# Three stages on one core: products in another order, two shared PSUM banks, other distances between the streams

## The chip, the core and the metric

The kernel runs on one core of a Trainium2 chip. The metric is the device time of one execution in microseconds (us), lower is better. A profile shows one further execution with every instruction's start and end. TensorE (PE) multiplies, and its weight loads (PEld) run beside it; VectorE (DVE), ScalarE (ACT) and GpSimd (POOL) do the elementwise work, the first two of them also out of PSUM, the matmuls' target of eight banks; SyncE (SP) issues all DMAs. Each engine takes its instructions in a fixed order, and semaphores make it wait for others.

## What is computed

Eight sequences of 576 tokens pass three stages. All tensors are float32.

```python
# 1: attention in chunks of 64 tokens, 8 heads of 64
scores = scale * np.matmul(q_c, k_c.transpose(0, 1, 2, 4, 3))
attn = softmax(scores); x = attn @ v_c            # -> x: (8, 576, 512)
# 2: gated block
h = np.maximum(x @ w_in, 0.0)
u, v = (h[..., :d_ff // 2], h[..., d_ff // 2:])
v_s = np.einsum('ts,bsd->btd', w_spatial, layernorm(v)) + b_spatial[None, :, None]
x = (u * v_s) @ w_out
# 3: a low-rank mix over the tokens, then two channel products
u = x + (x.transpose(0, 2, 1) @ U @ V).transpose(0, 2, 1)
out = u + np.maximum(u @ w_ch1, 0.0) @ w_ch2      # 512 -> 2048 -> 512
```

## The kernel before

Every float32 operand is split into a high and a low float16 part, and a product is three matmuls (`mm3`, lines 167 to 169): high by high, high by low, low by high. So TensorE's rows of almost every stage have these three lines, and the output tile tells them apart.

The work runs in four streams of Python generators. `gen_attn` takes 27 turns of attention (the first 9 run earlier by `gen_first`): scores into a tile `sp`, softmax, a transpose by DMA (`pt<-ph`), the second product into a tile `o`. `gen_moe(b)` does the gated block and the token mix of batch b. In PSUM tiles named `pb` it has, per batch, four or five v products of 512 columns (into `rz`), eight u products, eight spatial products and eight output products of 288 columns, four u stages of the low-rank mix (`tr`, into `ast`) and eight v stages (L762): four for the first part of the batch's tokens, which complete slice b of the channel stage, and four for the rest, which go to slice b + 1. After each, DVE adds (L763), ACT casts (L766) and POOL makes the low part (L767). `gen_sums(j)` forms, when slice j is complete, four sums of quarters of it (DVE L834 to L839, ACT L840, POOL L841), once for each half `kk` of its rows. `gen_quads` decodes packed weights for the channel stage, beside slice 0 only.

`gen_ch(j)` is the channel stage on slice j of 512 tokens, nine slices in all. Its first product is done as seven products of quarters (numbers 1 to 7, each six matmuls of 256 columns) instead of eight, with the sums as operands of 4 to 7. A slice has eight groups; in each, products 1, 6 and 2 go to the tile `pa` (one bank), and 5, 7, 3 and 4 to `pc` (one bank). ACT and DVE read them between the products (`q_e`, `q_v`, `q_z`) and make the hidden tile (L892, L893). Its second product, 24 matmuls of 512 columns into the four tiles `acc`, belongs to the group before and follows the seven. At a slice's end DVE reads `acc` into `ot` tiles (L942, L945; two buffers), ACT scales, and DMAs bring them out.

What sets the order is `Flow`: it runs the streams by an estimated clock. A stream that yields "pe" advances the clock and stays back by its pace times that cost; "wait" keeps it back for some ns, "need" until an event. The streams added first go first; the channel stage is last and fills what is left. A scheduler then places the instructions on each engine in the order that its own estimate gives, so the final order is not that of the code alone. A tile whose bank is in use by an earlier tile, or whose bank another engine still reads, waits.

PSUM before: four banks for `acc`, `pa` and `pc` one each (tags h0, h1), one for all `pb` tiles of the later batches (h2; `banks[0] = (2,)` before the streams start), and one for attention (pool `ps_a`).

Of the kernel before, what the change touches and what calls it, by code (L numbers as in the profile page):

```python
# [28 lines left out]

EARLY = (0, 0, 0, 0, 2, 1, 1)  # L30
FIRST_AT = 4
PACE_B = 0.8
PACES = (0.0, 0.0, 1.0, 1.0, 1.0, 1.0, 0.9, 0.9)
# [4 lines left out]
WA, WB, WC = 2500.0, 5500.0, 2500.0  # L38
# [54 lines left out]
def moe_kernel(  # L93
# [19 lines left out]
    ps_a = ctx.enter_context(tc.tile_pool(name="ps_a", bufs=1, space=PSUM))  # L113
# [4 lines left out]
    def b_psum(b):  # L118
        n = banks[0][banks[1] % len(banks[0])]
        banks[1] += 1  # L120
        return ps_h.tile([128, 512], F32, tag=f"h{n}", name="pb")
# [3 lines left out]
    NQ = NF // 2  # L125
# [404 lines left out]
    def gen_first(lo, hi):  # L530

        for i in range(lo, hi):
# [14 lines left out]
            tp = ps_a.tile([128, 4, 128], F32, tag="a", name="tp")  # L547
# [20 lines left out]
    def gen_attn(lo, hi):  # L568
# [5 lines left out]
        for i in range(lo, hi):  # L574
# [5 lines left out]
            sp = ps_a.tile([128, H, 64], F32, tag="a", name="sp")  # L580
# [20 lines left out]
            o = ps_a.tile([128, 4, 128], F32, tag="a", name="o")  # L601
# [21 lines left out]
    def gen_moe(b):  # L623
# [146 lines left out]
        for m in range(4):  # L770
# [17 lines left out]
            if m >= 1:  # L788
                if nxt == 2:
                    u_stage(m - 1)  # L790
                yield "pe", mmcost(128, 9)
            if m >= 2:
                v_stage(m - 2, 0, n1, b, 64 * b)
                yield "pe", mmcost(n1)
            yield "gap", 0
# [7 lines left out]
        for m in range(3, 4):  # L803
            v_stage(m, 0, n1, b, 64 * b)
            yield "pe", mmcost(n1)
        fl.done(("s", b, 0), 2500.0)
# [3 lines left out]
        for m in range(4):  # L810
            v_stage(m, n1, S - n1, b + 1, 0)
            yield "pe", mmcost(S - n1)
        fl.done(("s", b, 1), 2500.0)
# [10 lines left out]
    def gen_sums(j):  # L824
# [8 lines left out]
        for kk in range(2):  # L833
# [8 lines left out]
            yield "wait", 3000.0  # L842
        fl.done(("t", j), 3000.0)
# [7 lines left out]
    def gen_ch(j):  # L851
# [18 lines left out]

        for g in range(NQ + 1):
            n = j * NQ + g
            if g < NQ:
                if j == 0:
                    yield "need", ("wq", g)
                w = ws1_s[n % 3].rearrange("p a t (k m) -> p a t k m", k=2)
# [19 lines left out]

                product(1, pa[:, 0, :], True)
                nc.scalar.copy(out=q_e, in_=pa[:, 0, :])
                yield "pe", PQ
# [3 lines left out]
                product(5, pc[:, 0, :], True)  # L903
                add(q_v, pc[:, 0, :], q_e)
                yield "pe", PQ
                product(7, pc[:, 1, :], False)
                add(q_z[:, 2 * N2:3 * N2], pc[:, 1, :], q_v)
                yield "pe", PQ
                product(2, pa[:, 0, :], False)
# [3 lines left out]
                add(q_z[:, 0:N2], pc[:, 0, :], q_e)  # L913
                yield "pe", PQ
                product(4, pc[:, 1, :], False)
                w_load(0, n + 3)
                add(q_z[:, N2:2 * N2], pc[:, 1, :], q_e)
                parts(slice(N2, 4 * N2), q_z)
                yield "pe", PQ
            if g > 0:  # L920
                n -= 1
                w = ws2_s[n % 3]
                hd = hid_s[n % 2].rearrange("p a (f n) -> p a f n", f=2)
# [162 lines left out]
```

## Time and profile before

| | before |
|---|---|
| timed runs | 1480.81 and 1481.4 us, median 1481.11 |
| the profiled execution | 1483.17 us; span from first to last instruction 1481.4 us |
| mean granted TensorE clock | 0.933 of full |
| busy, share of the span | PE 1290.7 us (87%), DVE 770.9 (52%), POOL 593.1 (40%), ACT 561.7 (38%) |
| DMA | 185.47 MB, mean 125 GB/s |

PEclk is the granted clock of TensorE as a share of 2.4 GHz; it has two levels, 1.0 and 0.5, and a value between them is a mean over the stretch. Matmuls overlap in the profile: a row lasts longer than the distance to the next.

### The profile page before, as it was taken

The numbers are of one execution on the slowest core, as the hardware profiler recorded it, in microseconds if no ns is written. First come the engines' busy times: TensorE is split into PE (matmuls) and PEld (weight loads), VectorE is DVE, ScalarE is ACT, GpSimd is POOL, SyncE is SP. The second block draws the span as 40 slices with busy tenths as digits, with TensorE's granted clock in tenths as the row PEclk, the third lists the DMA queues.
The fourth block names the chain that finished last, engine by engine and source line by source line (L and its number), as shares of the span: only waits on it lengthen the run. The fifth ranks groups of instructions, "written<-read, shape, count | busy, mean of one in ns | idle before, by whom it ended". The sixth has DMA issues, their size and how long they took to land.

```text
span 1481.4 us, 24105 instructions
## 1 busy us (share of the span) xinstructions
PE 1290.7 (87%) x9604; PEld 869.6 (59%) x9604; DVE 770.9 (52%) x1427; ACT 561.7 (38%) x1127; POOL 593.1 (40%) x670
## 2 busy tenths in 40 slices
PE   8876688787899879997999699979996999589897
PEld 6564365554577637764776367746773676355554
DVE  6898877767634553446254635363325332733423
ACT  6665455444524532443245424333123212311111
POOL 3767686655615561545145525133113211500000
PEclk6897799888999979999999799989997999799999
DMA  8447443645434722562246313522333124234431
GB/s 263 132 141 232 135 130 123 198 127 182 137 115 143 177 73 86 148 151 105 83 128 163 109 65 100 146 94 82 104 102 91 65 93 127 90 118 139 149 118 43
DMA packets 119768, 185.47 MB, mean 125 GB/s; under 512 B 76132, under 2 KB 76772, under 8 KB 119656
## 3 DMA queue, kind: packets, MB, share of 16 engines
q1 hardware_dynamic: 119656, 183.93, 40.8%
q8 instruction: 75, 1.23, 0.3%
q14 instruction: 37, 0.30, 0.1%
HBM read 145.89 MB, written 20.97 MB: 113 GB/s over the span
## 4 chain that ended last, share of the span: by engine, by line
PE 53%; DVE 9%; POOL 5%; ACT 4%; DMA 3%; issue 2%; SPq 0%; ACTq 0%; POOLq 0%; DVEq 0%
PE acc L167 7%; PE acc L168 7%; PE acc L169 7%; PE pb L167 5%; PE pb L168 5%; PE pb L169 5%; PE pc L167 3%; PE pc L169 3%; PE pc L168 3%; PE pa L167 2%; PE pa L168 2%; PE pa L169 2%; POOL big L841 2%; DVE big L889 2%; DMA out_dram<-ot 2%
## 5 line engine op out<-in xcount | busy, mean ns | idle before, releaser
L889 DVE TENSOR_TENSOR big<-pc,big 128x256 f32<-128x256 f32 x288 | 121.5, 422 | 286.4 <-PE pc L169 282.0
L168 PEld LDWEIGHTS <-big 128*128 128x128 f16 x1584 | 156.3, 99 | 137.0 <-issue 51.9
L168 PE MATMUL acc<-big 128*128 128x512 f16 x576 | 219.1, 380 | 1.6 <-DVE big L893 1.5
L167 PEld LDWEIGHTS <-big 128*128 128x128 f16 x1584 | 156.2, 99 | 107.5 <-issue 29.9
L169 PE MATMUL acc<-big 128*128 128x512 f16 x576 | 218.6, 380 | 0.0
L169 PEld LDWEIGHTS <-big 128*128 128x128 f16 x1584 | 156.4, 99 | 86.3 <-issue 16.2
L167 PE MATMUL acc<-big 128*128 128x512 f16 x576 | 186.8, 383 | 4.7 <-ACT big L892 2.6
L167 PE MATMUL pc<-big 128*128 128x256 f16 x576 | 158.9, 276 | 26.3 <-DVE big L889 25.9
L169 PE MATMUL pc<-big 128*128 128x256 f16 x576 | 159.1, 276 | 0.0
L168 PE MATMUL pc<-big 128*128 128x256 f16 x576 | 158.9, 276 | 0.0
L719 POOL TENSOR_TENSOR gt<-g,gt 128x288 f16<-128x288 f32 x64 | 49.9, 781 | 240.7 <-ACT gt L718 240.3
L167 PE MATMUL pa<-big 128*128 128x256 f16 x432 | 120.5, 279 | 16.6 <-ACT big L840 7.5
L168 PE MATMUL pa<-big 128*128 128x256 f16 x432 | 120.2, 278 | 10.1 <-POOL big L841 9.0
L169 PE MATMUL pa<-big 128*128 128x256 f16 x432 | 120.4, 279 | 0.0
L893 DVE SCALAR_TENSOR_TENSOR big<-big 128x768 f16<-128x768 f32 x72 | 76.5, 1063 | 50.2 <-ACT big L892 50.0
L405 POOL TENSOR_TENSOR vbd<-vf,vbd 64x512 f16<-64x512 f32 x54 | 65.3, 1209 | 60.5 <-ACT vbd L404 52.9
L783 POOL TENSOR_TENSOR tr<-x,tr 128x64 f16<-128x64 f32 (+1 forms) x56 | 42.8, 785 | 114.7 <-ACT tr L780 66.2
L167 PE MATMUL pb<-gt,w 128*128 128x288 f16 x256 | 76.4, 298 | 14.1 <-DVE ast L751 5.1
L767 POOL TENSOR_TENSOR big<-x,big 128x512 f16<-128x512 f32 (+7 forms) x64 | 56.9, 896 | 77.5 <-ACT big L766 64.5
L892 ACT ACTIVATE big<-big 128x768 f16<-128x768 f32 x72 | 60.6, 842 | 68.2 <-DVE big L889 67.8
L167 PE MATMUL pb<-sp_m,vn 128*128 128x288 f16 x256 | 74.6, 291 | 13.4 <-DVE g L715 10.5
L892 ACT ACTIVATE big<-pa 128x256 f16<-128x256 f32 x72 | 27.5, 381 | 144.0 <-PE pa L169 135.1
(204 smaller groups left out, 3021.2 us busy)
## 6 DMA issues: line engine op xcount, KB each, us to landing
big<-wd SPq DMA_DIRECT2D x64, 896.0 KB, 4.7
big<-wd SPq DMA_DIRECT2D x64, 512.0 KB, 3.6
st<-in_wk_dram SPq DMA_DIRECT2D x36, 512.0 KB, 3.9
out_dram<-ot SPq DMA_DIRECT2D x32, 256.0 KB, 2.1
wd<-big SPq DMA_DIRECT2D x8, 896.0 KB, 4.3
vf<-in_v_dram SPq DMA_DIRECT2D x27, 256.0 KB, 2.8
qk<-in_q_dram SPq DMA_DIRECT2D x27, 256.0 KB, 2.7
qk<-in_k_dram SPq DMA_DIRECT2D x27, 256.0 KB, 3.3
```

The costliest lines, as they stand in the source:

```text
L167: nc.tensor.matmul(out=o, lhsT=wh, rhs=xh, start=start, stop=False, skip_group_check=more)
L168: nc.tensor.matmul(out=o, lhsT=wh, rhs=xl, start=False, stop=False, skip_group_check=more)
L169: nc.tensor.matmul(out=o, lhsT=wl, rhs=xh, start=False, stop=stop, skip_group_check=more)
L405: nc.gpsimd.tensor_tensor(out=vbd[r, 1, :, :, c, :], in0=vf[r], in1=vbd[r, 0, :, :, c, :], op=ALU.subtract)
L719: nc.gpsimd.tensor_tensor(out=gt[:, 1, m, c], in0=g, in1=gt[:, 0, m, c], op=ALU.subtract)
L767: nc.gpsimd.tensor_tensor(out=buf[:, 1, m, c], in0=x2[:, m, t], in1=buf[:, 0, m, c], op=ALU.subtract)
L783: nc.gpsimd.tensor_tensor(out=th[:, o0:o0 + n], in0=x2[:, m, t0:t0 + n], in1=th[:, t0:t0 + n], op=ALU.subtract)
L841: nc.gpsimd.tensor_tensor(out=ts[:, 1, :, kk, :], in0=t, in1=ts[:, 0, :, kk, :], op=ALU.subtract)
L889: nc.vector.tensor_tensor(out=o, in0=p, in1=y, op=ALU.add)
L892: nc.scalar.activation(out=hd[:, 0, c], in_=p, func=ACTF.Relu)
L893: nc.vector.scalar_tensor_tensor(out=hd[:, 1, c], in0=p, scalar=0.0, in1=hd[:, 0, c], op0=ALU.max, op1=ALU.subtract)
```

## The change

Within a group of the channel stage the products now come as 1, 5, 6, 7, then three of the eight pieces of the second product of the group before, then 2, 3, 4, and then the other five pieces. The adds on `pc` stand behind products 7 and 4, so that no read of a bank lies between two products into it. Attention has no bank of its own any more: while three banks are in turn for the gated block, attention takes h3; from the first group of slice 0 on, h2 and h3 go round for attention and gated block together. The pace of the batches goes from 0.8 to 1.0 down to 0.6, each v stage and u stage is followed by a wait of 600 ns, the wait between an attention turn's transpose and its second product goes from 5500 to 7500 ns, and the sums wait longer before the slice counts as ready.

```diff
+WV = 600.0
-PACE_B = 0.8
-PACES = (0.0, 0.0, 1.0, 1.0, 1.0, 1.0, 0.9, 0.9)
+PACE_B = 0.6
+PACES = (0.0, 0.0, 0.6, 0.6, 0.6, 0.6, 0.6, 0.6)
-WA, WB, WC = 2500.0, 5500.0, 2500.0
+WA, WB, WC = 2500.0, 7500.0, 2500.0
...
-    ps_a = ctx.enter_context(tc.tile_pool(name="ps_a", bufs=1, space=PSUM))
...
-    def b_psum(b):
+    def bank(shape, name):
         n = banks[0][banks[1] % len(banks[0])]
         banks[1] += 1
-        return ps_h.tile([128, 512], F32, tag=f"h{n}", name="pb")
+        return ps_h.tile(shape, F32, tag=f"h{n}", name=name)
+
+    def b_psum(b):
+        return bank([128, 512], "pb")
+
+    def a_psum(shape, name):
+        if len(banks[0]) == 3:
+            return ps_h.tile(shape, F32, tag="h3", name=name)
+        return bank(shape, name)
...
-            sp = ps_a.tile([128, H, 64], F32, tag="a", name="sp")
+            sp = a_psum([128, H, 64], "sp")
...
-            o = ps_a.tile([128, 4, 128], F32, tag="a", name="o")
+            o = a_psum([128, 4, 128], "o")
...
             if m >= 2:
                 v_stage(m - 2, 0, n1, b, 64 * b)
                 yield "pe", mmcost(n1)
+                yield "wait", WV
...
-            yield "wait", 3000.0
-        fl.done(("t", j), 3000.0)
+            yield "wait", 4500.0
+        fl.done(("t", j), 4000.0)
...
+        def second(n, start, stop, lo, hi):
+            w = ws2_s[n % 3]
+            hd = hid_s[n % 2].rearrange("p a (f n) -> p a f n", f=2)
+            for i in range(lo, hi):
+                f, m = divmod(i, 4)
+                mm3(acc[m], w[:, f, 0, m, :], w[:, f, 1, m, :], hd[:, 0, f, :], hd[:, 1, f, :],
+                    start and f == 0, stop and f == 1)
+                yield "pe", mmcost(512, 3)
...
                 if j == 0:
                     yield "need", ("wq", g)
+                    banks[0] = (2, 3)
...
                 product(1, pa[:, 0, :], True)
                 nc.scalar.copy(out=q_e, in_=pa[:, 0, :])
+                yield "pe", PQ
+                product(5, pc[:, 0, :], True)
                 yield "pe", PQ
                 product(6, pa[:, 1, :], False)
                 add(q_e, pa[:, 1, :], q_e)
                 yield "pe", PQ
-                product(5, pc[:, 0, :], True)
+                product(7, pc[:, 1, :], False)
                 add(q_v, pc[:, 0, :], q_e)
-                yield "pe", PQ
-                product(7, pc[:, 1, :], False)
                 add(q_z[:, 2 * N2:3 * N2], pc[:, 1, :], q_v)
                 yield "pe", PQ
+                if g > 0:
+                    yield from second(n - 1, g == 1, False, 0, 3)
                 product(2, pa[:, 0, :], False)
                 parts(slice(0, N2), pa[:, 0, :])
                 yield "pe", PQ
                 product(3, pc[:, 0, :], False)
-                add(q_z[:, 0:N2], pc[:, 0, :], q_e)
                 yield "pe", PQ
                 product(4, pc[:, 1, :], False)
                 w_load(0, n + 3)
+                add(q_z[:, 0:N2], pc[:, 0, :], q_e)
                 add(q_z[:, N2:2 * N2], pc[:, 1, :], q_e)
...
             if g > 0:
-                n -= 1
...
+                yield from second(n - 1, g == 1, g == NQ, 3 if g < NQ else 0, 8)
+                w_load(1, n + 2)
...
-    banks[0] = (2,)
```

The scheduler's result at two places. First DVE at the hand-over from slice 5 to slice 6, before: `ot` are the evacuations of slice 5, L834 and L836 to L839 the sums for slice 6, L763 the adds of batch 6's v stages, 128 columns for the first part and 448 for the rest.

```order
L942 SCALAR_TENSOR_TENSOR ot_11769<-big_72,acc0_10483 128x512
L942 SCALAR_TENSOR_TENSOR ot_11774<-big_72,acc1_10484 128x512
...
L763 SCALAR_TENSOR_TENSOR x2_11359<-pb_11697,x2_11359 128x128
L942 SCALAR_TENSOR_TENSOR ot_11779<-big_72,acc2_10485 128x512
L834 TENSOR_TENSOR big_72<-big_72 128x1024
L751 SCALAR_TENSOR_TENSOR ast_11361<-pb_11730,ast_11361 32x128
L942 SCALAR_TENSOR_TENSOR ot_11784<-big_72,acc3_10486 128x512
...
L763 SCALAR_TENSOR_TENSOR x2_11359<-pb_11751,x2_11359 128x128
```

The same stretch of DVE in the changed kernel, where the line numbers are higher (L846 for L834, L771 for L763, L911 and L915 for L889 and L893):

```order
L771 SCALAR_TENSOR_TENSOR x2_11254<-pb_11652,x2_11254 128x128
L771 SCALAR_TENSOR_TENSOR x2_11254<-pb_11800,x2_11254 128x448
L915 SCALAR_TENSOR_TENSOR big_69<-big_69 128x768
L771 SCALAR_TENSOR_TENSOR x2_11254<-pb_11805,x2_11254 128x448
L846 TENSOR_TENSOR big_69<-big_69 128x1024
L771 SCALAR_TENSOR_TENSOR x2_11254<-pb_11823,x2_11254 128x448
L911 TENSOR_TENSOR big_69<-pa_11661,big_69 128x256
```

There the second sum (this L846) and the last first-part add (128 columns) stand among the products of slice 5's last groups, ahead of all four evacuations of slice 5; before, they stood behind them.

TensorE at the same hand-over, before: `pb<-v4,ast` are v stages, `pa` is the new slice's first product, `pb<-w4,xT` the next batch's v product.

```order
L748 MATMUL pb_11663<-tr_11360,u_h_104 128x128
...
L762 MATMUL pb_11682<-v4_106,ast_11361 128x128
...
L762 MATMUL pb_11751<-v4_106,ast_11361 128x128
...
L762 MATMUL pb_11789<-v4_106,ast_11361 128x448
...
L167 MATMUL pa_11915<-big_72 128x256
...
L167 MATMUL pb_11817<-w4_93,xT_9405 128x512
```

And in the changed kernel, where `pa_11661` still belongs to slice 5's last group and `pa_11814` to slice 6:

```order
L770 MATMUL pb_11652<-v4_103,ast_11256 128x128
...
L770 MATMUL pb_11800<-v4_103,ast_11256 128x448
...
L175 MATMUL pa_11661<-big_69 128x256
...
L770 MATMUL pb_11841<-v4_103,ast_11256 128x448
...
L175 MATMUL pb_11863<-w4_90,xT_9405 128x512
...
L175 MATMUL pa_11814<-big_69 128x256
...
L175 MATMUL pc_11815<-big_69 128x256
```

The v stages moved ahead of a whole group of slice 5 and of tiles of batch 7. Second, TensorE in a lone group of slice 8, before; `pa` and `pc` with the higher number belong to the next group, and each row stands for the six (or four) matmuls of its product:

```order
L169 MATMUL acc3_13792<-big_72 128x512
...
L167 MATMUL pa_14256<-big_72 128x256
...
L167 MATMUL pc_14257<-big_72 128x256
...
L167 MATMUL pa_14334<-big_72 128x256
...
L167 MATMUL pc_14335<-big_72 128x256
...
L167 MATMUL acc0_13789<-big_72 128x512
```

In the changed kernel the tiles come in the same turn, but the 12 matmuls of `pc` stand together, first 3 and 4, then, behind the next group's product 1, 5 and 7; before, product 1 of the next group stood between 3 and 4, and the rest of product 2 between 7 and 3:

```order
L175 MATMUL pa_14253<-big_69 128x256
...
L175 MATMUL pc_14254<-big_69 128x256
...
L175 MATMUL pa_14331<-big_69 128x256
...
L175 MATMUL pc_14332<-big_69 128x256
...
L175 MATMUL acc0_13786<-big_69 128x512
```

## Rows read from the trace of the kernel before

**Rows 1.** Windows: span, each engine's busy time (instructions), PEclk, DMA share, GB/s
```profile
160.00:360.00 200.00, 154.47 (x1259) 103.75 (x1258) 151.14 (x247) 98.12 (x191) 133.68 (x125) 0.89 0.48 147
500.00:540.00 40.00, 25.27 (x202) 14.41 (x200) 24.52 (x43) 18.84 (x38) 24.34 (x22) 0.79 0.43 115
540.00:640.00 100.00, 99.91 (x851) 71.16 (x850) 43.62 (x94) 39.70 (x81) 42.92 (x56) 1.00 0.38 116
640.00:700.00 60.00, 50.30 (x336) 30.31 (x334) 31.41 (x64) 21.29 (x43) 27.00 (x36) 0.94 0.40 109
780.00:860.00 80.00, 65.32 (x518) 41.11 (x515) 44.71 (x86) 36.77 (x74) 44.64 (x53) 0.89 0.44 120
960.00:1020.00 60.00, 52.19 (x313) 30.33 (x312) 32.08 (x67) 21.28 (x42) 26.67 (x42) 0.91 0.30 98
1120.00:1160.00 40.00, 26.61 (x145) 13.93 (x144) 23.23 (x49) 14.03 (x26) 18.93 (x28) 0.79 0.23 69
1260.00:1300.00 40.00, 22.64 (x136) 13.42 (x134) 28.63 (x48) 15.24 (x28) 21.66 (x17) 0.74 0.28 86
1312.00:1377.00 65.00, 59.99 (x385) 37.32 (x384) 20.50 (x41) 8.27 (x18) 0.00 (x0) 1.00 0.41 132
```

**Rows 2.** Timeline of PE at the hand-over near 1130: start, length, instruction [idle <-releaser]
```profile
1128.53 0.29 PE L762 MATMUL pb<-v,ast 128*128 128x128 f16 x1 [4.00 <-DVE ast L751]
...
1133.96 0.37 PE L167 MATMUL pa<-big 128*128 128x256 f16 x1 [1.01 <-ACT big L840]
...
1137.06 0.37 PE L168 MATMUL pa<-big 128*128 128x256 f16 x1 [0.66 <-POOL big L841]
...
1144.24 0.27 PE L167 MATMUL pa<-big 128*128 128x256 f16 x1
```

**Rows 3.** Timeline of DVE, ACT and POOL at the same hand-over
```profile
1119.39 1.34 DVE L942 SCALAR_TENSOR_TENSOR ot<-big,acc 128x512 f32<-128x512 f16 x2 [3.98 <-PE acc L169]
...
1126.32 0.69 DVE L942 SCALAR_TENSOR_TENSOR ot<-big,acc 128x512 f32<-128x512 f16 x1 [2.50 <-DMA out_dram<-ot]
...
1140.81 1.05 ACT L840 CAST big<-big 128x1024 f16<-128x1024 f32 x1 [0.23 <-DVE big L839]
...
1141.93 2.12 POOL L841 TENSOR_TENSOR big<-big 128x1024 f16<-128x1024 f32 x1 [0.24 <-ACT big L840]
```

**Rows 4.** Groups by line and shape: busy and mean ns, then idle before
```profile
L841 POOL TENSOR_TENSOR big<-big 128x1024 f16<-128x1024 f32 x18 | 41.5, 2303 | 29.2 <-ACT big L840 27.1 <-PE pc L169 2.1
...
L834 DVE TENSOR_TENSOR big<-big 128x1024 f32<-128x1024 f16 x18 | 24.9, 1386 | 3.9 <-POOL big L767 3.5
...
L840 ACT CAST big<-big 128x1024 f16<-128x1024 f32 x18 | 18.8, 1044 | 31.9 <-DVE big L839 31.9
```

**Rows 5.** Timeline of one lone group of the channel stage, PE, DVE, ACT
```profile
1427.34 1.02 PE L167 MATMUL acc<-big 128*128 128x512 f16 x4
...
1432.31 0.38 PE L169 MATMUL acc<-big 128*128 128x512 f16 x1
...
1432.52 0.38 PE L167 MATMUL acc<-big 128*128 128x512 f16 x1
...
1434.94 0.27 PE L167 MATMUL pc<-big 128*128 128x256 f16 x1 [0.30 <-DVE big L889]
...
1437.12 0.42 DVE L889 TENSOR_TENSOR big<-pc,big 128x256 f32<-128x256 f32 x1 [0.91 <-PE pc L169]
...
1437.60 0.27 PE L167 MATMUL pc<-big 128*128 128x256 f16 x1 [0.51 <-DVE big L889]
...
1437.64 0.84 ACT L892 ACTIVATE big<-big 128x768 f16<-128x768 f32 x1 [2.58 <-DVE big L889]
...
1438.53 1.02 PE L167 MATMUL acc<-big 128*128 128x512 f16 x4
```

**Rows 6.** Waits between 150 and 370: us in total, times, longest
```profile
ACT big L194 <- DMA st<-in_wk_dram: 16.0, 6, 6.8
...
PE pc L167 <- DVE big L889: 7.7, 7, 2.8
```

More of the change, by code (lines that the diff above doesn't have):

```diff
@@ L546, in gen_first @@
             yield "wait", 1500.0
-            tp = ps_a.tile([128, 4, 128], F32, tag="a", name="tp")
+            tp = a_psum([128, 4, 128], "tp")
             sef = se.rearrange("p h j -> p (h j)")
@@ L794, in gen_moe @@
                 yield "pe", mmcost(n1)
+                yield "wait", WV
             yield "gap", 0
@@ L805, in gen_moe @@
             yield "pe", mmcost(n1)
+            yield "wait", WV
         fl.done(("s", b, 0), 2500.0)
@@ L812, in gen_moe @@
             yield "pe", mmcost(S - n1)
+            yield "wait", WV
         fl.done(("s", b, 1), 2500.0)
@@ L920, in gen_ch @@
             if g > 0:
-                n -= 1
-                w = ws2_s[n % 3]
-                hd = hid_s[n % 2].rearrange("p a (f n) -> p a f n", f=2)
-                for f in range(2):
-                    for m in range(4):
-                        mm3(acc[m], w[:, f, 0, m, :], w[:, f, 1, m, :], hd[:, 0, f, :], hd[:, 1, f, :],
-                            g == 1 and f == 0, g == NQ and f == 1)
-                        yield "pe", mmcost(512, 3)
-                w_load(1, n + 3)
+                yield from second(n - 1, g == 1, g == NQ, 3 if g < NQ else 0, 8)
+                w_load(1, n + 2)
                 if j == 0:
```

## Prediction, made before the changed kernel was run

> **What bounds the kernel now.** I read the windows of the span first [rows 1]. In the channel phase (from 360 on) TensorE is the bound: between 540 and 640 it is busy 99.91 of 100 us at a granted clock of 1.00, and such stretches follow in each slice. So time is won only where TensorE stands still or runs at the lower of its two levels. Take for each window its span minus busy time times PEclk, as work lost. The six windows in which one slice of channel work hands over to the next lose 40 - 25.27 x 0.79 = 20.0, then 12.7, 21.9, 12.5, 19.0 and 23.3 us, together 109 us [rows 1]. In them the granted clock is a mean of 0.74 to 0.94, and the kernel's stretches without idle have 1.00: part of the loss is the idle time, part the work done at 1.2 GHz after it.
>
> The lone stretch after 1312, where only channel groups are left, is busy 59.99 of 65 us at clock 1.00 [rows 1]. The stretch from 160 to 360, where the weights are decoded beside slice 0, loses 200 - 154.47 x 0.89 = 62.5 us.
>
> Next the timeline at one hand-over, from slice 5 to slice 6 (of 0 to 8). TensorE's last first-part v stage of batch 6 (pb of 128 columns, m = 3) starts at 1128.53, after 4.00 us of waiting; the new slice's first product starts at 1133.96 on a wait, goes on at 1137.06 on a wait for GpSimd's L841, and the second half of its operand is taken at 1144.24 [rows 2]. DVE, ACT and POOL at that place show why [rows 3]: DVE evacuates the old slice from 1119.39 (L942), stands at 1126.32 on an output DMA for its buffer, and only behind that come the sums (L834 to L839), their cast (L840 at 1140.81) and their low part (L841, 1141.93 + 2.12 = 1144.05). So 15.5 us lie between the v stage and its operand, and TensorE has little to do in them.
>
> Last, one lone group [rows 5]. Its period is 1438.53 - 1427.34 = 11.19 us. Its own matmuls are 24 of 512 columns, 0.215 us apart (1432.31 to 1432.52), and 42 of 256 columns at half of that: 9.7 us. The other 1.5 us are stops: pc matmuls of one bank wait for DVE's read of that bank at 1434.94 (0.30 idle) and at 1437.60 (0.51), and acc waits for ACT's L892.
>
> **The change part by part.** No instruction is added or removed; TensorE's own work stays the same. What moves is order, so I price the three places.
>
> *Hand-overs.* What is needed between the last first-part v stage and the second half of the new operand: the v stage's add, cast and low part (below 2.5 us, by the nearest row: L840, of at least twice the columns, is 1.04 us), L834 1.39, four DVE steps of 256 columns at 0.42 (L889, same shape), L840 1.04, L841 2.30 [rows 4, 5]: 8.9 us where nothing stands ahead, 15.5 us as the rows show it crowded [rows 2, 3]. What TensorE has to do meanwhile I count from the order, matmul columns at 2.4 GHz. Before, at this hand-over, four v stages and one 12-matmul tile: 4.0 us. In the changed order the same v stage stands ahead of 24 acc matmuls, two and a half groups of products and parts of two tiles of batch 7: 15.7 us. The six hand-overs have 11.2, 7.2, 11.7, 14.8, 15.7 and 13.6 us in this count (the second has 11.8 until the low part is asked for). The DVE rows move alike: before, the evacuation L942 with its DMA wait stands in front of both sums; in the changed order, both sums stand in front of it at five of the six hand-overs. Only at the first (slice 1 to 2) does the second sum stay behind all four evacuations. So I leave 8 us lost at the first, 5 at the second, 4 at each other: 29 us. Gain 109 - 29 = 80. Bounds: 1.5 us each left (one trip through DVE and back, of the size of the waits in [rows 2]) makes 100; half of the loss staying makes 55.
>
> The price of pulling batches ahead is cover: once batch j+1 is done, the rest of slice j runs alone, as lone groups do. By the order only one or two groups per slice stand so, and they pay 0.45 us each by the next step: inside the 4 us. The attention turn has 2 us more between its transpose and its second product; it waits for a DMA, and where that came late TensorE stood with it, so this can only give.
>
> *Lone groups.* With the new order, product 5 follows 1 and 7 follows 5 without a read between them. One stop is left: product 5 needs both adds on pc, which now stand behind product 4. By the row at 1437.12 and its neighbours [rows 5]: the last matmul's end 0.16 us behind its slot, 0.03 to DVE, two adds of 0.42, 0.06 back, minus product 1, which lies between (6 x 0.108 = 0.65): 0.44 us. The first acc needs ACT's 0.84 behind these adds, and products 5 and 7 (1.3 us) cover it. Product 3 needs the reads after 7: 20 acc matmuls (4.3 us) stand between. Period 9.7 + 0.45 = 10.2 us, so 1.0 us for each of the 16 lone groups: 16 us. Bounds: 0 if the stop moves whole to another bank, 24 if none is left.
>
> *Weight phase.* Batch 1 now has three banks until slice 0 begins and starts ahead of it by 10 us of TensorE work, and DVE's order gives the decoding the same place. In the waits of this stretch, weight DMAs held ACT 16.0 us, and products waited 7.7 us for reads of pc [rows 6]. The decoding sets the pace, so I take half of the 7.7, 4 us, with 0 and 12 as bounds on this side, and a loss of 10 on the other if pulling batch 1 forward holds a decoded weight up.
>
> *Two shared banks.* Instead of one bank for attention and one for the gated block, two go round. A tile waits for the reader of the tile before the last instead of the last. With one bank, 540 to 640 shows no idle [rows 1]; a second cannot make that better there. Nothing.
>
> Sum: 80 + 16 + 4 = 100 us off the profiled span of 1481.4, which with what lies around it took 1483.17; the two timed runs have a median of 1481.11, so I take 1481 - 100 = 1381.
>
> **The rivals.** *Hand-overs half open*: the sums come earlier in the order, but DVE, ACT and POOL, each in order, still give them late, as the 15.5 us against 8.9 show can be. For it: the cover at the second hand-over (7.2 us) is below even 8.9. Against it: elsewhere it is above, and the output wait no longer stands in front. 1381 + 40 = 1421.
>
> *Sharing costs, and the kernel gets slower.* In a round of two, attention's tiles (27 turns, 2 tiles each) sit between the tiles of the batches. If a score tile is read late, because the softmax stands behind sums on DVE, the second batch tile behind it waits, and TensorE, in order, with it. Some 338 tiles go round (40.5 for each of seven batches, by the loops, and 54). At 0.30 us for each the whole gain of 100 is gone; at 0.5 us it is 169: 1381 + 169 = 1550. Against it: a tile of 12 matmuls of 288 columns lasts 1.5 us, and a read of 256 columns takes 0.42 [rows 5], so one tile in between covers a prompt reader.
>
> *The clock falls in the full stretches too.* Where TensorE has many short stops the granted clock falls, as in the window 160 to 360 (0.89) [rows 1]. If going round two banks makes such stops all through the 900 us of channel work beside batches (360 to 1260), at 0.89: 900 / 0.89 - 900 = 111 us, 1381 + 111 = 1492. Against it: 540 to 640 already alternates banks at 1.00. The Trainium skill, TensorE: Matmul & The Clock Gate, section "A second HAM failure mode: psum-queue depth-cycling", says that a kernel cycling through PSUM banks had idles so frequent that its clock kept falling and rising. By that rule the case here would come true; no trace shows it beside full work.
>
> *Decoding is held up*: the weight phase grows by 20 us, all else as forecast: 1401, inside the range.
>
> **How the numbers follow.** Forecast, 1381, chance 0.77 with the decoding case. Half open, 1421: 0.13. Clock, 1492: 0.03. Sharing: 0.03 at 1550 and 0.04 with a smaller wait per tile, around 1481. Downwards the bounds give 20 more at the hand-overs and 8 in each of the other parts, of which I take 31 together: 1350. Upwards the half-open case with the weight phase's loss of 10 gives 1431. Range 1350 to 1431. Two per cent, about what a measurement tells from no change, is 30 us: below 1451 is faster, chance 0.77 + 0.13 = 0.90; between 1451 and 1511, 0.03 + 0.04 = 0.07; above, 0.03.
>
> **What would show it.** Right: windows at the hand-overs with TensorE above 90% and clock near 1.00; DVE's sums ahead of the evacuations in time; a lone period of 10.2 us with one wait of pc on DVE; the stretch from 160 to 360 no more than 12 us shorter or longer. Wrong: pb, sp or o waiting for readers within slices, lone groups at 11 us, or sums that start where they started. What would make the forecast wrong most likely is that the engines behind the sums are later than the order says.

## The result

The changed kernel takes 1369.72 us (two runs, 1369.63 and 1369.82) against 1481.11 before: 0.925 of the time, with a 95% interval of 0.921 to 0.929. The forecast was 1381 in a range of 1350 to 1431. The profiled execution has a span of 1368.0 us. The page of the kernel after begins so (busy time; then busy tenths and clock in 40 slices):

```profile
PE 1256.7 (92%) x9604; PEld 866.9 (63%) x9604; DVE 769.1 (56%) x1427; ACT 565.3 (41%) x1127; POOL 588.0 (43%) x670
...
PE   8887579876999989999999999999999999989998
...
PEclk6798789998999999999999999999999999999999
```

Behind the first third there is hardly a slice below 9 in either line. Windows of the kernel after, as in [rows 1] (span, then each engine's busy time, PEclk, DMA share, GB/s); the hand-overs come earlier in time now:

```profile
160.00:360.00 200.00, 159.36 (x1329) 108.60 (x1328) 162.89 (x256) 103.72 (x199) 139.91 (x129) 0.91 0.54 157
500.00:540.00 40.00, 32.37 (x190) 18.47 (x189) 29.02 (x56) 15.34 (x28) 23.57 (x35) 0.91 0.26 89
540.00:640.00 100.00, 99.89 (x904) 73.54 (x903) 46.41 (x92) 44.23 (x92) 44.67 (x44) 1.00 0.50 142
640.00:680.00 40.00, 37.43 (x229) 22.25 (x228) 26.34 (x56) 15.26 (x28) 17.61 (x35) 1.00 0.33 108
780.00:820.00 40.00, 36.53 (x225) 21.32 (x224) 29.35 (x63) 15.91 (x30) 25.26 (x35) 1.00 0.36 113
900.00:940.00 40.00, 40.00 (x268) 25.20 (x267) 22.51 (x49) 12.63 (x26) 12.87 (x16) 1.00 0.43 142
1040.00:1080.00 40.00, 40.00 (x253) 24.34 (x251) 23.65 (x51) 14.42 (x26) 16.78 (x24) 1.00 0.41 135
1160.00:1200.00 40.00, 38.53 (x259) 24.59 (x258) 24.12 (x48) 11.97 (x22) 7.64 (x7) 1.00 0.48 162
1200.00:1220.00 20.00, 14.35 (x75) 8.34 (x73) 15.38 (x22) 6.99 (x12) 10.39 (x8) 0.83 0.30 99
```

By the same sum as in the prediction (span minus busy time times PEclk) the hand-overs now lose 40 - 32.37 x 0.91 = 10.5, then 2.6, 3.5, 0, 0, and 1.5 + 8.1 us in the last two windows: 26 us where 109 were lost. The middle ones have no idle time at all. The 8.1 us at 1200 are new; below they get a cause of their own.

The hand-over from slice 5 to slice 6, which [rows 2, 3] show of before, is this in the kernel after (timelines of PE, DVE, ACT and POOL; start, length, instruction, idle and its releaser):

```profile
1044.25 0.41 PE L770 MATMUL pb<-v,ast 128*128 128x128 f16 x2
...
1037.11 1.23 DVE L846 TENSOR_TENSOR big<-big 128x1024 f32<-128x1024 f16 x1 [0.93 <-POOL big L775]
...
1047.52 1.21 DVE L846 TENSOR_TENSOR big<-big 128x1024 f32<-128x1024 f16 x1
...
1064.43 1.33 DVE L960 SCALAR_TENSOR_TENSOR ot<-big,acc 128x512 f32<-128x512 f16 x2 [2.21 <-PE acc L177]
...
1052.76 2.13 POOL L853 TENSOR_TENSOR big<-big 128x1024 f16<-128x1024 f32 x1 [5.40 <-ACT big L852]
```

The two sums (L846, the old L834) run 27 and 17 us before the old slice's evacuation (L960, the old L942); before, they came after it. From the v stage to the end of the low part it is 1054.89 - 1044.25 = 10.6 us, where it was 15.5, and TensorE works on slice 5 meanwhile.

A lone group, as in [rows 5], has one stop left (PE, two neighbouring groups):

```profile
1327.48 0.27 PE L175 MATMUL pc<-big 128*128 128x256 f16 x1 [0.19 <-DVE big L911]
...
1337.60 0.27 PE L175 MATMUL pc<-big 128*128 128x256 f16 x1 [0.19 <-DVE big L911]
```

The period is 1337.60 - 1327.48 = 10.12 us, after 11.19.

DVE's first read of `acc` in each slice gives the gain by place. Before: 367.3, 511.9, 671.8, 823.7, 977.8, 1119.4, 1270.8, 1383.5 us and the end at 1481.4; after: 363.2, 503.7, 647.9, 794.2, 932.9, 1064.4, 1190.4, 1281.1 and 1368.0. So the slices are shorter by 4.1 (weights), 4.1, 15.7, 5.6, 15.4, 10.1, 25.4, 22.0 and 11.0 us. That is 113.4 us. The three places that the forecast names make some 104 of them: 83 at the hand-overs, 17 in the lone groups (16 times 1.07) and 4 beside the weights. The other 9 lie outside the three. What the forecast said of the parts of the edit is another matter, and the runs below are about that.

### The profile page after: what moved, and what is told of

Its sections match the earlier page's. It is cut to its first block, busy times and chain, and to the rows that moved or that the text cites. A ratio compares the mean times of both kernels' runs of the same rounds, so it can differ in the third digit from the quotient of the medians.

```text
span 1368.0 us, 24028 instructions
## 1 busy us (share of the span) xinstructions
PE 1256.7 (92%) x9604; PEld 866.9 (63%) x9604; DVE 769.1 (56%) x1427; ACT 565.3 (41%) x1127; POOL 588.0 (43%) x670
## 4 chain that ended last, share of the span: by engine, by line
PE 65%; DVE 18%; POOL 5%; DMA 4%; ACT 4%; issue 3%; SPq 0%; DVEq 0%; POOLq 0%; ACTq 0%
PE acc L176 7%; PE acc L175 7%; PE acc L177 7%; PE pb L175 7%; PE pb L176 7%; PE pb L177 7%; PE pc L175 4%; PE pc L177 4%; PE pc L176 4%; PE pa L175 3%; PE pa L176 2%; PE pa L177 2%; DVE big L911 2%; DVE big L249 1%; DVE big L915 1%
## 5 line engine op out<-in xcount | busy, mean ns | idle before, releaser
L176 PE MATMUL acc<-big 128*128 128x512 f16 x576 | 218.3, 379 | 2.5 <-DVE big L915 2.5
L177 PE MATMUL acc<-big 128*128 128x512 f16 x576 | 218.3, 379 | 0.0
L175 PE MATMUL acc<-big 128*128 128x512 f16 x576 | 201.8, 382 | 2.6 <-ACT big L914 1.8
L911 DVE TENSOR_TENSOR big<-pc,big 128x256 f32<-128x256 f32 x288 | 114.9, 419 | 37.7 <-PE pc L177 33.6
L175 PE MATMUL pa<-big 128*128 128x256 f16 x432 | 118.6, 275 | 15.7 <-DVE big L911 8.5
L176 PE MATMUL pa<-big 128*128 128x256 f16 x432 | 118.8, 275 | 0.0
L177 PE MATMUL pa<-big 128*128 128x256 f16 x432 | 118.6, 275 | 0.0
L915 DVE SCALAR_TENSOR_TENSOR big<-big 128x768 f16<-128x768 f32 x72 | 75.2, 1045 | 43.3 <-ACT big L914 43.1
L915 DVE SCALAR_TENSOR_TENSOR big<-pa,big 128x256 f16<-128x256 f32 x72 | 30.4, 422 | 121.0 <-ACT big L914 120.7
L400 POOL TENSOR_TENSOR qbd<-qk,qbd 64x512 f16<-64x512 f32 x54 | 66.5, 1231 | 49.9 <-ACT qbd L399 45.8
L775 POOL TENSOR_TENSOR big<-x,big 128x512 f16<-128x512 f32 (+7 forms) x64 | 51.8, 815 | 76.8 <-ACT big L774 66.7
L175 PE MATMUL pb<-xT,w 128*128 128x288 f16 x256 | 74.8, 292 | 10.8 <-DVE x L771 4.7
```

The source lines that it names most:

```text
L175: nc.tensor.matmul(out=o, lhsT=wh, rhs=xh, start=start, stop=False, skip_group_check=more)
L176: nc.tensor.matmul(out=o, lhsT=wh, rhs=xl, start=False, stop=False, skip_group_check=more)
L177: nc.tensor.matmul(out=o, lhsT=wl, rhs=xh, start=False, stop=stop, skip_group_check=more)
L400: nc.gpsimd.tensor_tensor(out=qbd[r, 1, :, c, :], in0=qv[r], in1=qbd[r, 0, :, c, :], op=ALU.subtract)
L775: nc.gpsimd.tensor_tensor(out=buf[:, 1, m, c], in0=x2[:, m, t], in1=buf[:, 0, m, c], op=ALU.subtract)
L911: nc.vector.tensor_tensor(out=o, in0=p, in1=y, op=ALU.add)
```

## The experiments

Three groups of lines can be taken out of the change one by one: **the products** (their order, the reads placed last, the second product split), **the banks** (two shared ones, and the batches' third bank kept until slice 0) and **the times** (`PACES`, `PACE_B`, `WB`, `WV`, the waits in `gen_sums`). With them all eight combinations were run. Each is compared with runs of before on the same chip (1479 to 1480 us there).

### The products alone

```diff
+                product(5, pc[:, 0, :], True)
+                yield "pe", PQ
                 product(6, pa[:, 1, :], False)
...
-                product(5, pc[:, 0, :], True)
...
+                if g > 0:
+                    yield from second(n - 1, g == 1, False, 0, 3)
```

> The kernel before with the new product order alone (products alternate banks, reads last, second product split round them); bank for attention, single bank for the batches and all waits and paces as before. Theory A, place of the sums: the loss at hand-overs follows from whether DVE's sums for the next slice stand ahead of the evacuations of the old one. In this kernel's order they do so at every hand-over (the scheduler moved them because products' reads moved), so the hand-overs should fill although no time or pace was changed: lone period 10.1 us (16 us off) and 70 to 90 us at the hand-overs, 1375 to 1400 us. Theory B, each part as its name says: the products give only the lone groups, 1481 - 16 = 1465, with hand-over windows as busy as before (25 to 34 us of 40). Theory C, it takes the second bank to fill the hand-overs: the sums come early but the v stages wait for the one bank's readers, 1420 to 1450.

Measured: 1513.75 us, 1.023 of before (1.021 to 1.025). No theory had it slower. The expectation also misread the order: in DVE's order the sums counted up to each evacuation were compared one slice off. Read rightly, three sums stand ahead of the first evacuation where the next slice needs four, four of six ahead of the second, and so on: the next slice's sums stand behind, not ahead.

### The change without one of its parts

Without the products (the old order in the changed kernel):

> The changed kernel with the product order of before; shared banks, paces and waits stay as changed. Sums stand ahead of the evacuations at all hand-overs (both of them, at the first too). Theory A: hand-overs stay filled, lone period back to 11.2 us, 16 lone groups: 1370 + 17 = 1387, less up to 8 us for the first hand-over: 1379 to 1390. Theory B: the same, 1386. A rival in which the product order itself fills the hand-overs (TensorE pays a stop per group also where the batches run beside it): 1400 or more.

Measured: 1416.48 us, 0.957 (0.956 to 0.959): 46 us above the whole change, not 17. Without the times:

```diff
-PACE_B = 0.6
-PACES = (0.0, 0.0, 0.6, 0.6, 0.6, 0.6, 0.6, 0.6)
+PACE_B = 0.8
+PACES = (0.0, 0.0, 1.0, 1.0, 1.0, 1.0, 0.9, 0.9)
...
-WA, WB, WC = 2500.0, 7500.0, 2500.0
+WA, WB, WC = 2500.0, 5500.0, 2500.0
```

(and without the `WV` waits, with 3000 in `gen_sums`):

> The changed kernel with paces and waits of before; product order and shared banks stay as changed. In DVE's order the sums fall back behind the evacuations at three hand-overs (out of slices 0, 2 and 4; from slice 1 on the pattern is nearly that of before, 0 or 1 sum ahead at two of them). Theory A: the loss comes back there: 1370 + 45 to 75 = 1415 to 1445, lone period still 10.1 us. Theory B (times worth about 80): 1450. Theory C, two banks fill the hand-overs wherever the sums stand: 1370 to 1385.

Measured: 1405.10 us, 0.950 (0.948 to 0.951), 10 us under the least that theory A gives and 20 over the most of theory C: neither. Without the banks:

```diff
+    ps_a = ctx.enter_context(tc.tile_pool(name="ps_a", bufs=1, space=PSUM))
...
+        return ps_a.tile(shape, F32, tag="a", name=name)
...
-                    banks[0] = (2, 3)
...
+    banks[0] = (2,)
     fl.add(gen_quads(3, NQ))
```

> The changed kernel with attention in a bank of its own and one bank for the batches' v tiles in the channel phase; products, paces and waits as changed. Sums stand ahead at all hand-overs. Theory A: nothing changes, 1362 to 1375. Theory C: the second bank is needed at the hand-overs or in the stretches, 1400 or more, with waits of pb for DVE's or GpSimd's reads. Rival the other way: sharing cost 0.1 us or more per tile in the changed kernel, so 1335 or less.

Measured: 1508.49 us, 1.019 (1.017 to 1.022). With everything else of the change in it, the kernel without the banks is slower than before. (The sentence on its sums has the same misreading as in the first run: they stand behind.) So the part that the prediction gave nothing decides. Its windows at the hand-overs:

```profile
500.00:540.00 40.00, 26.02 (x182) 14.40 (x182) 23.15 (x41) 17.01 (x34) 27.02 (x32) 0.74 0.36 94
660.00:700.00 40.00, 27.95 (x172) 15.88 (x171) 19.11 (x39) 14.86 (x31) 21.49 (x28) 0.74 0.27 73
820.00:880.00 60.00, 37.94 (x273) 22.27 (x273) 36.34 (x66) 24.67 (x49) 38.08 (x50) 0.83 0.24 65
980.00:1020.00 40.00, 26.01 (x154) 14.98 (x153) 21.25 (x39) 13.39 (x29) 16.60 (x20) 0.83 0.24 71
1120.00:1180.00 60.00, 41.40 (x250) 24.43 (x248) 24.72 (x47) 18.25 (x42) 20.40 (x27) 0.83 0.27 72
1280.00:1340.00 60.00, 35.42 (x199) 21.71 (x197) 30.96 (x50) 18.47 (x40) 24.74 (x22) 0.66 0.26 64
```

They lose 20.7, 19.3, 28.5, 18.4, 25.6 and 36.6: 149 us, more than the 109 of before. The last of them, in the timelines of PE and DVE of the same kernel:

```profile
1288.96 0.38 PE L176 MATMUL acc<-big 128*128 128x512 f16 x1
...
1299.24 0.21 PE L769 MATMUL pb<-v,ast 128*128 128x64 f16 x1 [3.13 <-DVE ast L758]
...
1314.17 0.24 PE L769 MATMUL pb<-v,ast 128*128 128x64 f16 x1 [0.70 <-DVE ast L758]
...
1287.43 1.33 DVE L958 SCALAR_TENSOR_TENSOR ot<-big,acc 128x512 f32<-128x512 f16 x2 [4.15 <-PE acc L176]
...
1311.23 1.23 DVE L845 TENSOR_TENSOR big<-big 128x1024 f32<-128x1024 f16 x1 [0.75 <-POOL big L774]
```

The old slice is finished at 1289, while four output tiles, four u stages and all four first-part v stages of the batch (1299 to 1314) are still to come. They run with nothing beside them, each waiting for the last one's readers. DVE isn't what is late: it takes the first sum (L845) 1.3 us after the start of the v stage that this sum still needed (the third, at 1309.93). The batch is.

That gave a new theory, **the lead**: the TensorE work which the order puts between a batch's last first-part v stage and the first product of the slice that it completes. It is counted from each kernel's order of instructions, matmul columns at 2.4 GHz; negative where the first product stands ahead. All eight combinations, with the lead into the slices 2 to 7:

```
parts in it                us       of before   lead into slices 2, 3, 4, 5, 6, 7 (us)
none (before)              1480.07  1           -4.7  -6.9   -9.7  -6.8  -10.4   -6.8
times                      1466.40  0.992      -11.1  -6.9   -7.1  -6.8   -8.9   -6.8
products                   1513.75  1.023       -4.5  -3.3  -20.4 -13.2  -17.9  -13.6
products, times            1508.49  1.019       -5.8  -3.3  -20.4 -13.2  -17.9  -15.1
banks                      1419.69  0.960       -1.3  17.2   -6.9   1.0   17.4    9.2
banks, times               1416.48  0.957        1.9  17.4    5.3  20.8   17.4   18.8
banks, products            1405.10  0.950       -1.4  -6.2  -10.4  -6.1   -0.6    6.7
all three (after)          1370.42  0.927       -5.6   0.5    0.2  12.9   14.2   12.6
```

(The rows come from three chips, so the ratios are to be compared. The last row is a second measurement of the changed kernel, beside the last runs below.)

Within one order of products the time goes with the leads, small differences apart. With the old products the six add up to -45, -48, 37 and 82 us at 1480, 1466, 1420 and 1416 us; with the new ones to -73, -76, -18 and 34 at 1514, 1508, 1405 and 1370. Across the two orders it doesn't: the banks with the times have the largest sum of the eight and are slower than the banks with the products. So the lead says whether a hand-over is filled, and not what the groups themselves cost. Two of these rows were run to test the theory. The banks alone:

> The kernel before with the two shared banks alone (and the third bank for the batches until slice 0 begins); products, paces and waits as before. Theory L, made after the first four runs: what counts at a hand-over is the lead, the TensorE work that its order puts between the batch's last first-part v stage (which completes the next slice) and that slice's first product. Before it is -4.7 to -10.4 us at the slices 2 to 7, in the kernel with attention in its own bank -3 to -20, in the changed kernel -5.6 to 14.2. Here it is -1.3, 17.2, -6.9, 1.0, 17.4 and 9.2: three hand-overs of six filled, so about half of the 109 us comes back although no pace was changed, with the lone period at 11.2 us and waits of pc as before: 1425 to 1445. Theory S (the banks are worth nothing by themselves): 1475 to 1485.

Measured: 1419.69 us, 0.960 (0.957 to 0.962), 5 us below the lower end. The banks alone are worth 60 us. They are two things at once, the two shared banks and the third one that batch 1 keeps until slice 0, and no run takes these apart. Slice 0's evacuation begins at 368.5 us in this kernel and at 367.3 before, so up to there the third bank has brought nothing. The times alone:

> The kernel before with the new paces and waits alone. Theory L: the leads are -11.1, -6.9, -7.1, -6.8, -8.9 and -6.8 us, as before or worse, so nothing is gained: 1475 to 1500. Theory B (the times are what fills the hand-overs, worth about 80): 1400.

Measured: 1466.40 us, 0.992 (0.990 to 0.993), 9 us below the theory's lower end and 66 above the rival: some 13 us that the leads don't explain, and not the 80.

### Is it the order, or the waits at the bank?

One bank could cost in two ways: on the chip, where each tile waits for the reader of the one before, or through the order, since the scheduler's own estimate counts those waits and puts the tiles of a batch further back. The next kernel has the two banks and a late order:

```diff
-PACES = (0.0, 0.0, 0.6, 0.6, 0.6, 0.6, 0.6, 0.6)
+PACES = (0.0, 0.0, 2, 2, 2, 2, 2, 2)
...
-WA, WB, WC = 2500.0, 7500.0, 2500.0
+WA, WB, WC = 2500.0, 5500.0, 2500.0
```

> The changed kernel with its two shared banks and its products, but its batches made late: pace 2 for 0.6 and the attention's wait 5.5 us as before the change. Leads at the slices 2 to 7: -3.9, -1.9, -23.8, -16.6, -17.9 and -9.9 us, like those of the kernel with attention in its own bank (-5.8, -3.3, -20.4, -13.2, -17.9, -15.1), which took 1508 us; that one stays negative in its order even at pace 0. Theory L, the bank works through the lead alone: the hand-overs are lost again, 1470 to 1510. Theory W, the bank works by waits on the chip (with one bank each tile waits for the reader of the tile before; with two it doesn't): late batches cost less, 1400 to 1430. In between, both: 1430 to 1470.

Measured: 1484.33 us, 1.003 (1.001 to 1.004), inside the theory of the lead. Its last hand-over's window, and PE there:

```profile
1260.00:1320.00 60.00, 37.64 (x243) 24.10 (x241) 32.38 (x50) 20.34 (x44) 25.80 (x24) 0.77 0.30 72
```

```profile
1284.86 0.23 PE L754 MATMUL pb<-tr,u_h 128*128 128x128 f16 x1 [1.74 <-DMA tr<-tr]
...
1288.68 0.27 PE L754 MATMUL pb<-tr,u_h 128*128 128x128 f16 x1 [2.20 <-DMA tr<-tr]
...
1290.89 1.14 PE L770 MATMUL pb<-v,ast 128*128 128x64 f16 x3 [1.09 <-DVE ast L759]
...
1301.71 0.37 PE L175 MATMUL pc<-big 128*128 128x256 f16 x1 [6.86 <-ACT big L852]
```

The window loses 31 us though two banks go round: in these rows the chain's own steps (the transpose's DMA, `ast`, the sums) are waited for. Over the six hand-overs this kernel loses 27.5, 13.3, 27.7, 12.1, 13.6 and 31.0, together 125 us by its windows, the kernel with its own banks 149; the leads add up to -74 and -76. So about five sixths of that loss come with the late order, and some 24 us are left for the waits at the one bank. This is an attribution by two kernels, not a measurement of the waits alone, but a row of waits agrees with it. A v stage that waits for the add of the tile before it waits for the bank. That row, for the kernel before, the one with its own banks and the late one with two (TensorE's waits: total, times, longest):

```profile
PE pb L762 <- DVE x L763: 27.8, 24, 3.2
```

```profile
PE pb L769 <- DVE x L770: 29.5, 29, 3.8
```

```profile
PE pb L770 <- DVE x L771: 3.6, 7, 0.8
```

With two banks nearly all of this wait is gone, and the late kernel is slow without it.

### Further ahead, and the wait at 1211

```diff
-PACE_B = 0.6
-PACES = (0.0, 0.0, 0.6, 0.6, 0.6, 0.6, 0.6, 0.6)
+PACE_B = 0.5
+PACES = (0.0, 0.0, 0.5, 0.5, 0.5, 0.5, 0.5, 0.5)
...
-WA, WB, WC = 2500.0, 7500.0, 2500.0
+WA, WB, WC = 2500.0, 9500.0, 2500.0
```

> The changed kernel with its batches a little further ahead still: pace 0.5 for 0.6 and the attention's second wait 9.5 us for 7.5. Leads at the slices 2 to 7: 5.7, 12.7, 10.6, 14.2, 18.7 and 12.4 us, where the changed kernel has -5.6, 0.5, 0.2, 12.9, 14.2 and 12.6; both sums ahead of the evacuations at every hand-over. Theory L: of the 16 us that the changed kernel still loses at the first three of these (10.0, 2.6 and 3.5 by its windows) 8 to 14 come back, less some 0.45 us for each of up to 10 more groups that then run alone: 1355 to 1364. Rival, the hand-overs have given what they can: 1368 to 1372, or more if batches that are further ahead find no free buffer.

Measured: 1376.88 us, 0.931 (0.929 to 0.933): worse than the changed kernel. By windows of 20 us its hand-overs lose some 5 us less, but from 160 to 380 it loses 64 us where the changed kernel loses 55; the longer wait and the lower pace act beside the decoding too. Which of the two does it was not tried.

The new stop of the changed kernel stands in slice 7's third group. DVE, POOL and PE at that place:

```profile
1202.26 2.15 DVE L846 TENSOR_TENSOR big<-big 128x1024 f32<-128x1024 f16 x1
...
1204.34 0.41 DVE L911 TENSOR_TENSOR big<-pc,big 128x256 f32<-128x256 f32 x1
1204.67 1.03 DVE L848 TENSOR_TENSOR big<-big 128x256 f32<-128x256 f32 x1
1205.63 1.37 DVE L849 TENSOR_TENSOR big<-big 128x256 f32<-128x256 f32 x1
...
1203.41 5.88 POOL L873 TENSOR_TENSOR us<-big 128x512 f32<-128x512 f16 x4
...
1211.45 0.37 PE L175 MATMUL pa<-big 128*128 128x256 f16 x1 [5.18 <-DVE big L915]
```

While GpSimd adds the last slice's residual, DVE's sums take 1.03 to 1.37 us instead of 0.42, and the group's reads stand behind them. In the next kernel a copy of one column makes each of GpSimd's additions wait for a hidden tile of slice 8:

```diff
-            for m in range(4):
-                o = us[:, m, 0:SLICE]
-                nc.gpsimd.tensor_tensor(out=o, in0=x[:, 0, m, :], in1=x[:, 1, m, :], op=ALU.add)
...
+            if last and 1 <= g <= 4:
+                o = us[:, g - 1, 0:SLICE]
+                nc.gpsimd.tensor_copy(out=us[:, g - 1, 0:1], in_=hid_s[(n - 1) % 2][:, 0, 0:1])
+                nc.gpsimd.tensor_tensor(out=o, in0=x[:, 0, g - 1, :], in1=x[:, 1, g - 1, :], op=ALU.add)
```

> The changed kernel with GpSimd's four additions for the last slice's residual (128x512, 5.9 us, which run at 1203 in the changed kernel beside DVE's sums for slice 8) held back into slice 8's groups by a one-column copy from each group's hidden tile. Theory: they are what stretches DVE's sums at 1202 to 1211 (L848 to L851 1.25 us instead of 0.42) and with them the reads of slice 7's third group, so the wait of 5.2 us of pa for DVE and the time at half clock behind it go: 5 to 9 us less, 1361 to 1365. Rival: the sums stand before the reads whatever GpSimd does: 1368 to 1371. Later, four groups of slice 8 have GpSimd beside DVE's reads: up to 3 us back.

Measured: 1365.17 us, 0.924 (0.922 to 0.925), at the upper end of the theory's range. In its trace the same places read:

```profile
1206.36 0.41 DVE L848 TENSOR_TENSOR big<-big 128x256 f32<-128x256 f32 x1
1206.69 0.41 DVE L849 TENSOR_TENSOR big<-big 128x256 f32<-128x256 f32 x1
...
1209.89 0.27 PE L175 MATMUL pa<-big 128*128 128x256 f16 x1 [1.93 <-DVE big L916]
```

The sums are back at 0.41 us and the wait falls from 5.18 to 1.93. The changed kernel was not run on that chip, so the 5 us were measured once more on another chip, beside the changed kernel and with a lower pace for the batches. The changed kernel there:

> The changed kernel as it is, beside the next three on one chip: 1364 to 1372 us, the span's windows as in its first profile.

Measured: 1370.42 us, 0.927 (0.926 to 0.929). With the lower pace:

> The changed kernel with pace 0.4 for 0.6 for batches 2 to 7 only; the attention's wait and batch 1's pace, and with them the stretch of the weights, stay as changed. Leads at the slices 2 to 7: 2.2, 14.7, 15.4, 15.2, 29.7 and 20.1 us. Theory L with what the run with everything further ahead showed (its hand-overs lost 6 us less in all, its weight stretch 8 us more): the weight stretch stays within 2 us of the changed kernel, the hand-overs lose 5 to 10 us less, some 8 more groups run alone at 0.45 us each: 1360 to 1367. Rival, further ahead costs as much as it brings: 1368 to 1374.

Measured: 1368.36 us, 0.925 (0.924 to 0.927), 2 us below the changed kernel with overlapping intervals: the rival. Its weight stretch loses 54 us as expected, its hand-overs less, and small stops at other places take most of that back. With the lower pace and GpSimd's additions held back:

> The same pace of 0.4, and GpSimd's additions for the last slice held back into its groups as in the run before. If the two gains lie at different places they add up: 5 us below the kernel with the pace alone and 8 to 13 below the changed kernel, 1354 to 1362. If the pace moves slice 8's sums to a place where the additions don't meet them, no more than the pace alone.

Measured: 1362.75 us, 0.921 (0.920 to 0.923): 7.7 us below the changed kernel on the same chip, the intervals apart. Two of its windows:

```profile
500.00:540.00 40.00, 37.19 (x259) 22.89 (x257) 28.43 (x56) 18.29 (x34) 23.03 (x36) 0.97 0.37 121
...
1160.00:1220.00 60.00, 56.05 (x374) 36.19 (x372) 36.17 (x68) 16.59 (x29) 12.25 (x8) 1.00 0.48 162
```

The first hand-over now loses 3.9 us (10.5 in the changed kernel), the last stretch 4.0 (9.6). It is the fastest version here; by the steps, 2 us come from the pace, with overlapping intervals, and 5.6 from holding GpSimd's additions back.

## Why the prediction was right, and which step was not

**Hand-overs.** 29 us were to be left of 109, 26 are: 83 gained, 80 forecast. The order of TensorE's work as it stood in the changed kernel was enough to forecast the place. The first hand-over, where the second sum stays behind the evacuations, is the worst of them as the step said (10.5 us for 8). At the hand-overs into the slices 3 to 6, 6.1 us are left instead of 17. The sum hides errors at single hand-overs that cancel; that it came within 3 us is in part luck. At the end the step missed a new wait: the sums for slice 8 come so early that GpSimd's residual meets them (8.1 us).

**Lone groups.** 10.2 us forecast, 10.12 measured, with the one wait that the step left, pc for DVE behind product 4. But the 16 us are the worth of the product order at the end of the program only. With the banks and the times in place the order of products is worth 46 us (1416.48 to 1370.42, on two chips), with the banks alone 15, without the banks it costs 34. Part of the 46 shows in the rows on pc of the kernel that has the old products beside the new banks and times, and of the changed kernel (waits of PE: total, times, longest):

```profile
PE pc L175 <- DVE big L902: 41.1, 59, 4.3
```

```profile
PE pc L175 <- DVE big L911: 9.0, 25, 2.3
```

Once batches are ahead, each slice ends in groups that run alone, and each of those pays the old stops. The prediction named these groups and gave them the new order's price, 0.45 us each inside the 4 us of a hand-over; what the old order would have made them pay stood in no term. Why the products alone make the leads worse (-20 at slice 4) was not tried; the order shows that they do.

**Weight phase.** 4 us forecast; slice 0's evacuation begins 4.1 us earlier, and between 150 and 370 the products' waits for reads of pc fall from 7.7 to 3.9 us. That the one comes from the other isn't shown: the same evacuation begins at 340.9 us in the kernel with its own banks and at 373.8 in the one without the products.

**Two shared banks: nothing.** This step failed as an account of the parts. It asked whether a tile would wait less on the chip, looked at 540 to 640, where nothing waits [rows 1], and stopped there. Even for that question it was the wrong place. The 27.8 us that v stages wait for the one bank are the largest row of TensorE's waits in the whole kernel before, and 24.2 of them lie in the hand-overs. The larger part works before the program runs: with one bank the order has the tiles of a batch further back, and the batch ends behind its slice. Counted from that order, its leads stay negative even at pace 0, which wasn't run. That the scheduler's estimate of the waits at the bank is what moves the tiles is argued: the orders differ by the banks alone, but no run looks inside the scheduler. Alone the banks bring 60 us; taken out of the change they cost 138. The sum came out right because the gain was priced by place, from an order in which the banks' work was already done, while the text gave the banks nothing. Whoever had used the parts' prices to choose what to keep would have left out the one that carries the rest. The times alone are worth 13 us, on top of the two others 35.

**The place of the sums.** The prediction made the output wait in front of the sums the reason of the loss. The kernel with its own banks shows a hand-over where the evacuations were issued and done, and the first sum followed its v stage within 1.3 us: there the batch itself is late. The prediction's own rows point the same way: the output wait ends at 1126.32, and the v stage that the second sum needs starts only at 1128.53 [rows 2, 3]. Sums behind the evacuations are a sign of a late batch and not by themselves the cause. One price of this step was also too low: the four DVE steps behind L834 were taken at 0.42 us from another line, and their own lines (L836 to L839) average 0.58 to 0.67 in the kernel before. In the hand-over of [rows 3] the first of them for the second sum takes three times the price, beside an operation of GpSimd (DVE, then POOL, before):

```profile
1137.04 1.24 DVE L836 TENSOR_TENSOR big<-big 128x256 f32<-128x256 f32 x1 [1.22 <-POOL big L841]
...
1136.97 2.20 POOL L767 TENSOR_TENSOR big<-x,big 128x448 f16<-128x448 f32 x2
```

**The rivals.** Sharing that costs 0.30 us a tile: the reverse was true. The clock: 540 to 640 has 1.00 at 99.89 of 100 us busy, with the two banks going round between attention and batches. The Trainium skill, "TensorE: Matmul & The Clock Gate", section "A second HAM failure mode: psum-queue depth-cycling", tells of a kernel going round PSUM banks whose clock kept falling and rising; that didn't come true in this window. Half open: only the first hand-over is. Decoding held up: by windows of 20 us 55 us are lost from 160 to 380, 63 before; the run further ahead shows that it can happen, at 8 us.

## What to carry to other kernels

When a scheduler orders the instructions, a buffer or a PSUM bank has two prices: the waits on the chip, and the order that the scheduler makes because of it; a stretch of the trace without waits says nothing of the second, nor of waits at other places. Before pricing parts of an edit one by one, build the order of each part and count one quantity that the bound rests on (here the work left between a batch's end and its slice's need). Such a count shows which places fill; it doesn't replace the price of the work itself, and parts that only pay together can't be summed. And look at what comes early now: work that has moved forward meets whatever another engine does there.

## What the runs showed of the hardware

The steps of DVE's sums, 256 columns with both operands in SBUF, took 1.03 to 1.37 us beside GpSimd's additions, which last 5.88 / 4 = 1.47 us each, and 0.41 us where GpSimd stood still. The additions are held up as well: moved into slice 8's groups, one lasts 1.15 us.

```profile
1280.10 1.15 POOL L893 TENSOR_TENSOR us<-big 128x512 f32<-128x512 f16 x1
```

In the midst of the four additions of the changed kernel, at 1204.34, an addition of the same size with one operand in PSUM took its usual 0.41 us. The Trainium skill, "SBUF — State Buffer", section "SBUF: two separate sides", says that a DVE operation with two SBUF inputs and a GpSimd operation that reads SBUF exclude each other for a whole instruction; the trace agrees, in the size of the steps and in the one that isn't held up.

TensorE's clock came back with the work: 0.957 on average over the execution (0.933 before). In the kernel with its own banks the window 1280 to 1340, busy 35.42 of 60 us, ran at a mean of 0.66 of the higher level.
